# Attention, routed experts and a dense layer on one core: the first expert's first 128 slots are gathered within attention, and two of its h tiles take those slots in the slot chain

## The chip, the cores and the metric

The kernel runs on one core of a Trainium2 chip. The metric is device microseconds (us) of one execution, as a median of several runs. The engines are PE (TensorE: matmuls, and transposes by a matmul with the identity), DVE (VectorE), ACT (ScalarE), POOL (GpSimd) and SP (SyncE, which here issues DMAs). Each engine works through its own instructions in a fixed order and waits where an operand isn't there.

## The reference

All data is float32. There are 2304 tokens (4 sequences of 576), a model width of 512 (8 heads of 64), and 8 experts with an inner width of 1024.

```python
scores = (q @ k.T) / 8                     # per sequence and head
ret = (scores * gamma**(i - j) for i >= j) @ v
x = heads joined                           # 2304 x 512
logits = xn @ en.T / tau                   # rows and expert embeddings normalised
expert_idx = argmax(logits); gate = softmax(logits)[expert_idx]
for e in range(8):
    mask = expert_idx == e
    out[mask] = gate[mask] * (relu(x[mask] @ w1[e]) @ w2[e])
h = out @ w_in                             # second layer, 512 -> 2048
y = where(h > 0, h, exp(min(h, 0)) - 1) @ w_out
```

## The kernel before, in words

The program is one function, `tile_kernel`, in which the order on each engine is the order of the code: there is no scheduler. It has three stretches.

**Attention** runs over ten units `u` (0 to 9; `NU - 1` = 9 is the last one and is short). The output of a unit is one or two of the 18 token tiles `n` of 128 tokens. In a unit, PE makes the scores and values and a transposed output `xTp`; ACT copies it (`xT`, L395); PE turns it back and at the same time multiplies by the expert embeddings (`xa`, L444); DVE takes from `xa` the rows `xs`, which go by DMA to `xd` in DRAM, and the logits `lg` (L452 for the last tile, L460 for the others); ACT sums squares (`squares`, L478).

**Routing** is done in four groups of tiles, `GROUPS` = (first tile, count) = (0, 5), (5, 5), (10, 3), (13, 5). For each group `expert_steps` finds the winning expert of each token and its rank (`rp`, `pr`, L547) and `gate_steps` the gate (L588 to L599). `grouped` feeds a tile's steps in and `pump` deals them out between attention's instructions. For each tile `slots` (on POOL) makes a one-hot of the slot column (`o`, L609), one of the slot row (`Bt`, L610) and their products with token number and gate (`At`, L612). The first expert handled is that with the most tokens in the first two groups (`first`); its capacity is 342 slots, `CAPS[0]`, that of the others falls to 276.

**The slot chain** follows the last tile. PE multiplies `Bt` and `At` of all tiles into `pid` (token of each slot) and `pig` (gate of each slot): `begin` takes tiles 0 to 12, `finish` the last five. DVE reduces `pid` to `ids0` (shown as `ids`, L887), the list of the first expert's tokens, and POOL gathers their rows from `xd` with three indirect DMAs of 128, 128 and 96 rows (L945). Meanwhile `warm(8)` and `warm(4)` are matmuls on constants that nobody reads. `pig` then gives the gates (`gsl`), the three row blocks are scaled by them (`row`: blocks 0 and 2 on DVE L954, block 1 on ACT L956), PE transposes them (`tp`, L981), and they are split into a high and a low part, `xth` and `xtl`, because each fp32 product is made of three matmuls: high by high, low by high, high by low. Weights are split likewise: `ha`, `la` from the raw `ra` (first layer), `hb`, `lb` from `rb` (second layer); ACT makes the high part (L202), DVE the low (L207).

**The experts** are 64 steps `i`, eight an expert. `mm1` makes one h tile (128 of the 1024 inner units by up to 342 slots), L1003 for `i` = 0 and L233 for the others; ACT and DVE split it (`hh` L1008, `hl` L1009); `mm2` adds its product to the four accumulators `acc` (L1026, L1028). An h tile takes 12 matmuls in `mm1` and 12 in `mm2`, each as wide as the expert's capacity. After an expert the accumulators are copied into `ys` and sent to `yd`. The second layer follows, with products of summed and differenced blocks, and its own gathers and splits.

## Time and profile before

| what | value |
|---|---|
| time, median of 3 runs | 727.44 us (726.22 to 728.1) |
| the profiled execution's own time | 725.94 us |
| its span (first to last instruction) | 724.0 us |
| mean granted TensorE clock, of 1 | 0.992 |
| PE busy | 707.3 us, 98% of the span |
| PEld (weight loads) busy | 654.1 us, 90% |
| DVE busy | 589.3 us, 81% |
| ACT busy | 447.3 us, 62% |
| POOL busy | 260.5 us, 36% |

All start times in the rows are counted from the start of the span; the profiled execution's time is 1.94 us more than its span. The stretch of the change is from about 93 to 128 us: the last three attention units, the slot chain and the first h tiles.

### The profile page before, as it was taken

To read this page: it belongs to the slowest core of one execution; us is meant where nothing else is said; L and a number is where in the kernel's file an instruction comes from. 1 tells how busy PE (TensorE), PEld (TensorE's weight loads), DVE (VectorE), ACT (ScalarE), POOL (GpSimd) and SP (SyncE) were. 2 spreads that over 40 slices of the span, in tenths; PEclk is the share of its full clock that TensorE was granted. 3 is DMA by queue.
4 is the path that set the end of the run, shared out by engine and by line. 5 is a ranking of instruction groups with operands and counts; after the bars stand their busy time and mean duration, and the time that the engine had idled before them with its cause. 6 is when DMAs were issued, how large, how long until landed. Compare 5 with 4: busy or idle time off the path is not lost.

```text
span 724.0 us, 15526 instructions
## 1 busy us (share of the span) xinstructions
PE 707.3 (98%) x5940; PEld 654.1 (90%) x5940; DVE 589.3 (81%) x942; ACT 447.3 (62%) x690; POOL 260.5 (36%) x352
## 2 busy tenths in 40 slices
PE   8999979999999999999999999999999999999996
PEld 7988967999999999999989999889999989999985
DVE  4566789998888898789799999987779998777773
ACT  3443444656666666576777667776666778666572
POOL 3436643328483571003333222372112238111103
PEclk9999998999999999999999999999999999999998
DMA  7877656998999989795353311245211224211012
GB/s 211 230 218 223 170 171 211 314 348 271 359 284 326 327 270 307 239 348 159 106 176 109 110 59 59 69 165 167 67 59 58 84 90 142 64 59 59 29 30 87
DMA packets 101843, 123.66 MB, mean 171 GB/s; under 512 B 12250, under 2 KB 71934, under 8 KB 101766
## 3 DMA queue, kind: packets, MB, share of 16 engines
q1 hardware_dynamic: 98278, 112.62, 48.8%
q0 software_dynamic: 3104, 9.83, 3.8%
q8 instruction: 47, 0.77, 0.4%
q10 hardware_dynamic: 384, 0.19, 0.1%
q14 instruction: 30, 0.25, 0.1%
HBM read 99.78 MB, written 22.85 MB: 169 GB/s over the span
## 4 chain that ended last, share of the span: by engine, by line
PE 47%; issue 9%; POOL 1%; DMA 1%; DVE 0%; POOLq 0%; SPq 0%
PE o L233 20%; PE X L233 11%; PE Y L233 8%; PE h L233 3%; PE acc L1026 2%; PE acc L1028 1%; POOL out_dram L1474 1%; DMA qa<-wd 1%; POOL qs L1261 0%; POOL qa L1262 0%; POOL qs L1263 0%; DVE la('q', 20)_9470 L207 0%; PE tp L981 0%; POOLq L1558 0%; POOL qs L1264 0%
## 5 line engine op out<-in xcount | busy, mean ns | idle before, releaser
L1261 POOL TENSOR_TENSOR qs<-qa 128x256 f32<-128x256 f32 x24 | 23.6, 982 | 240.6 <-DMA qa<-wd 44.9
L233 PE MATMUL h<-xth,ha 128*128 128x332 f32 (+7 forms) x252 | 74.4, 311 | 0.1
L1026 PE MATMUL acc<-hh,lb 128*128 128x342 f32 (+7 forms) x256 | 73.5, 303 | 0.0
L1026 PE MATMUL acc<-hh,hb 128*128 128x342 f32 (+7 forms) x256 | 73.5, 304 | 0.0
L233 PE MATMUL h<-xtl,ha 128*128 128x332 f32 (+7 forms) x252 | 72.3, 303 | 0.0
L1008 ACT ACTIVATE hh<-h 128x342 fp32r<-128x342 f32 (+7 forms) x64 | 27.3, 426 | 52.2 <-PE h L233 50.8
L1425 ACT ACTIVATE rA<-hA 128x768 f32<-128x768 f32 x24 | 20.3, 848 | 50.4 <-DVE hA L1418 50.4
L1410 DVE TENSOR_TENSOR u<-Y,m 128x384 f32<-128x384 f32 x48 | 26.6, 554 | 28.0 <-PE Y L233 25.9
L207 DVE TENSOR_TENSOR la<-ra,ha 128x1024 fp32r<-128x1024 f32 x32 | 39.2, 1224 | 12.4 <-ACT ha L202 12.3
L1026 PEld LDWEIGHTS acc<-hh,lb 128*128 128x128 f32 x256 | 48.3, 189 | 0.0
L1026 PEld LDWEIGHTS acc<-hh,hb 128*128 128x128 f32 x256 | 48.2, 188 | 0.0
L233 PEld LDWEIGHTS h<-xth,ha 128*128 128x128 f32 x252 | 47.5, 189 | 0.6 <-issue 0.3
L233 PEld LDWEIGHTS h<-xtl,ha 128*128 128x128 f32 x252 | 47.6, 189 | 0.0
L945 POOL DMA_INDIRECT row<-xd,idsp x21 | 24.0, 1144 | 64.8 <-ACT xth L986 52.7
L1028 PE MATMUL acc<-hl,hb 128*128 128x342 f32 (+7 forms) x256 | 46.6, 304 | 0.4 <-DVE hl L1009 0.4
L233 PE MATMUL h<-xth,la 128*128 128x332 f32 (+7 forms) x252 | 45.6, 303 | 0.0
L1474 POOL DMA_INDIRECT out_dram<-ob,idc x18 | 21.2, 1178 | 66.6 <-ACT ob L1471 63.8
L207 DVE TENSOR_TENSOR lb<-rb,hb 128x1024 fp32r<-128x1024 f32 x32 | 39.4, 1233 | 3.7 <-ACT hb L202 3.5
L1028 PEld LDWEIGHTS acc<-hl,hb 128*128 128x128 f32 x256 | 39.0, 188 | 0.9 <-DVE hl L1009 0.9
L233 PEld LDWEIGHTS h<-xth,la 128*128 128x128 f32 x252 | 38.5, 188 | 0.0
L1442 ACT CAST ghB<-hB 128x768 fp32r<-128x768 f32 x24 | 20.0, 835 | 26.9 <-DVE hB L1438 26.9
L348 DVE TENSOR_TENSOR A<-sc,mask 128x512 f32<-128x512 f32 x32 | 20.6, 686 | 19.3 <-PE sc L342 19.3
(1693 smaller groups left out, 2343.2 us busy)
## 6 DMA issues: line engine op xcount, KB each, us to landing
ra<-in_moe_w_dram SPq DMA_DIRECT2D x32, 512.0 KB, 5.4
rb<-in_moe_w_dram SPq DMA_DIRECT2D x32, 512.0 KB, 5.6
qb<-wd SPq DMA_DIRECT2D x48, 256.0 KB, 2.9
draw<-in_moe_w_in_dram SPq DMA_DIRECT2D x16, 512.0 KB, 5.8
...
```

The lines of the kernel that those rows point to most:

```text
L207: nc.vector.tensor_tensor(out=lo, in0=src, in1=hi.bitcast(F32), op=ALU.subtract)
L233: nc.tensor.matmul(o, l, r, start=first and n_ == 0, stop=last and n_ == len(seq) - 1, skip_group_check=True)
L348: return vec.tensor_tensor(out=t[:, :, :w], in0=sc[j][:, :, :w], in1=m.unsqueeze(1).to_broadcast([P, 4, w]), op=ALU.mult)
L945: pool.indirect_dma_start(out=t[:m].rearrange("p k w -> p (k w)"), out_offset=None, in_=xd[:, :], in_offset=bass.IndirectOffsetOnAxis(ap=i ...
L1008: nc.scalar.activation(out=hh, in_=hp[:, :c], func=AF.Relu)
L1026: nc.tensor.matmul(acc[d][:, :c], w[d][w_], hh, start=f == 0 and w_ == 0, stop=False)
L1028: nc.tensor.matmul(acc[d][:, :c], w[d][0], hl, start=False, stop=f == 7)
L1261: pool.tensor_tensor(out=S1, in0=A21, in1=A22, op=ALU.add)
L1410: vec.tensor_tensor(out=S_[nm], in0=S_["Y"], in1=S_["m1"], op=ALU.add)
L1425: nc.scalar.activation(out=Q[n]["r" + z], in_=Q[n]["h" + z], func=AF.Relu, scale=-1.0)
L1442: nc.scalar.copy(out=Q[n]["gh" + z], in_=Q[n]["h" + z])
L1474: ins = pool.indirect_dma_start(out=out[:, :], out_offset=bass.IndirectOffsetOnAxis(ap=idc[:, col:col + 1], axis=0), in_=ob, in_offset=None)
```

## The change

Of the first expert's 342 slots the first 128, `EARLY`, can be filled from the first ten token tiles alone (`TEARLY` = 10, the first two groups), which are ranked long before the last tile. The changed kernel treats them apart:

- In unit 8 (`LAST - 1`) POOL marks the tokens of these slots (`early_slots`), PE multiplies (`pea`, ten matmuls of 5 columns), DVE reduces to `idsa` and `gsla`, and POOL gathers 128 rows, `rowa`, from the part of `xd` that the first ten tiles fill (`early_ids`).
- In unit 9 ACT scales `rowa` by the gates, PE transposes it, ACT makes its high part `xtha` (`early_turn`), and DVE, in the slot chain, its low part `xtla`.
- The first weight block's parts `ha`, `hb`, `la`, `lb` are made within attention and no longer in the slot chain and after it; `lb` is made on POOL. The loads of decoded weights (`decode_load`) and of the second raw block (`load_b(2)`) are issued later.
- In the slot chain PE computes the h tiles 0 and 1 for these 128 slots (`early1`) and their products with the second layer's weights (`early2`) into one bank `acce`. These 48 matmuls of 128 columns stand where 8 of the constant matmuls stood, before `rp`, and around the last tiles of `pid` and `pig`; `warm(8)` and `warm(4)` become `warm(4)` and `warm(3)`. `acce` is copied to `sume`.
- After the slot chain only two row blocks are gathered, of 128 and 96 rows; block 1 is scaled on DVE and block 2 on ACT. The early columns of `xth` and `xtl` are copied from `xtha` and `xtla` by ACT. `mm1` and `mm2` for `i` = 0 and 1 work on columns 128 to 341 (214 instead of 342); at the end of the first expert DVE adds `sume` to `ys`.

```diff
 SHORT = [c for _, c, _ in UNITS].index(-1)
 GROUPS = [(0, 5), (5, 5), (10, 3), (13, 5)]
 NPART = 5
+TEARLY = sum(GROUPS[GFIRST])
+EARLY = P
+FEARLY = 2
+assert EARLY * NE <= TEARLY * P
...
-    def split_low(w, u):
+    def split_low(w, u, eng=nc.vector):
         hi, lo, src = w[u]
-        nc.vector.tensor_tensor(out=lo, in0=src, in1=hi.bitcast(F32), op=ALU.subtract)
+        eng.tensor_tensor(out=lo, in0=src, in1=hi.bitcast(F32), op=ALU.subtract)
         w[u] = (hi, lo)
...
+    ea = {}
+    def early_slots():
+        f18 = st.tile([P, 1], F32, name="f18")
+        sel = st.tile([P, TEARLY], BF16, name="sel")
+        ea["ae"] = st.tile([P, TEARLY, NPART], BF16, name="ae")
+        pool.tensor_scalar(out=f18, in0=first, scalar1=float(NT), scalar2=None, op0=ALU.mult)
+        for gi in range(GFIRST + 1):
+            g0, gn = GROUPS[gi]
+            pool.tensor_scalar(out=sel[:, g0:g0 + gn], in0=gt[gi]["h"][:, 0, :gn], scalar1=f18, scalar2=None, op0=ALU.is_equal)
+        pool.tensor_tensor(out=ea["ae"], in0=sel.unsqueeze(2).to_broadcast([P, TEARLY, NPART]), in1=parts[:, :TEARLY, :], op=ALU.mult)
+    def early_ids():
+        p_ = ea["p"] = ps.tile([P, NPART], F32, tag="qT", name="pea")
+        for n in range(TEARLY):
+            nc.tensor.matmul(p_, Bt[:, n, :], ea["ae"][:, n], start=n == 0, stop=n == TEARLY - 1)
+        with nc.allow_low_precision(reason="whole numbers below 2304"):
+            vec.tensor_reduce(out=idsa, in_=p_[:, :2], axis=AX.X, op=ALU.add)
+        t = ea["row"] = dec.tile([P, DM], F32, tag="dsq", name="rowa", bufs=2)
+        pool.indirect_dma_start(out=t, out_offset=None, in_=xd[:TEARLY * P, :],
+                                in_offset=bass.IndirectOffsetOnAxis(ap=idsa, axis=0))
+        vec.tensor_reduce(out=gsla, in_=p_[:, 2:], axis=AX.X, op=ALU.add)
...
+    def early_turn():
+        pt = ea["pt"] = ps.tile([P, KD, P], F32, tag="kT", name="pta")
+        for kk in range(KD):
+            nc.tensor.transpose(pt[:, kk, :], ea["row"][:, kk * P:(kk + 1) * P], ident)
+        ea["xt"] = [dec.tile([P, KD, P], F32R, tag="dsq", name="xtha", bufs=2), dec.tile([P, KD, P], F32R, tag="db1", name="xtla", bufs=3)]
+        nc.scalar.copy(out=ea["xt"][0], in_=pt)
+    def spare_tile(tag, nm):
+        return ld.tile([P, H, 2, D], F32, tag="l" + tag, name=nm, bufs=4 if tag == "v" else 3).rearrange("p h s d -> p (h s d)")[:, :EARLY]
+    def early1(f, low):
+        if not low:
+            ea["hp", f] = ps.tile([P, 512], F32, tag="sc1", name="hea0") if f == 0 else ps.tile([P, 2, 512], F32, tag="Y", name="hea1")[:, 0]
+        hp = ea["hp", f][:, :EARLY]
+        xh, xl = ea["xt"]
+        w = tiles_a(f)
+        for l, r in ((0, xl),) if low else ((0, xh), (1, xh)):
+            for kk in range(KD):
...
+    def early_parts(f):
+        hp = ea["hp", f][:, :EARLY]
+        hh, hl = (spare_tile(t, f"e{x}{f}") for x, t in zip("hl", "qk"))
+        ea["h", f] = [hh.bitcast(F32R), hl.bitcast(F32R)]
+        nc.scalar.activation(out=ea["h", f][0], in_=hp, func=AF.Relu)
+        return lambda: vec.scalar_tensor_tensor(out=ea["h", f][1], in0=hp, scalar=0.0, in1=hh, op0=ALU.max, op1=ALU.subtract)
+    def early2(f, low):
+        if f == 0 and not low:
+            ea["acc"] = ps.tile([P, 2, 512], F32, tag="X", name="acce")[:, 0]
+        hh, hl = ea["h", f]
+        w = tiles_b(f)
+        for d in range(KD):
+            for w_, r in ((0, hl),) if low else ((0, hh), (1, hh)):
+                nc.tensor.matmul(ea["acc"][:, d * EARLY:(d + 1) * EARLY], w[d][w_], r, start=f == 0 and not low and w_ == 0 and d == 0,
+                                 stop=low and f == FEARLY - 1, skip_group_check=True)
+    def early_sum():
+        ea["sum"] = xr.tile([P, KD, EARLY], F32, name="sume")
+        vec.tensor_copy(out=ea["sum"], in_=ea["acc"].rearrange("p (k m) -> p k m", k=KD))
...
     held = None
+    LAST = NU - 1
     RANKED = 1 + [sum(GROUPS[GFIRST]) - 1 in ns for _, _, ns in UNITS].index(True)
     for u in range(NU):
         ns = UNITS[u][2]
...
+        if u == LAST:
+            nc.scalar.activation(out=ea["row"], in_=ea["row"], func=AF.Copy, scale=gsla)
         if held is not None:
             grouped(held)
+        if u == LAST - 1:
+            early_slots()
         if before is not None:
             xrows(before)
         if u < NU - 1 and u != SHORT:
         transposes(u + 1, 1)
         load(u + 3 if u else 2, "q" if u else "v", copied.get((u + 1, 1, "k")))
         if u == NU - 2:
+            split_of("a", 0, rawa[0], 1024, wa)
+        values(u)
+        load(u + 3, "k" if u else "q", copied[u, "x"])
+        if u == LAST - 1:
+            early_ids()
+        if u == LAST:
+            early_turn()
             decode_load(0)
...
         if before is not None:
             grouped(before)
+        if u == LAST - 1:
+            split_of("b", 0, rawb[0], 1024, wb)
         if u == NU - 1:
             while live:
...
         scores(u + 1, 0)
+        if u == LAST - 1:
+            split_low(wa, 0)
         xrows(ns[0], 2 if u == RANKED else 0)
         held = ns[0]
         for _ in range(8):
             if ready:
                 slots(*ready.pop(0))
+        if u == LAST - 1:
+            split_low(wb, 0, pool)
         if u < NU - 1:
             pump(1 if u == NU - 2 else 24, 0)
...
-    split_of("a", 0, rawa[0], 1024, wa)
+    early1(0, False)
     while live:
         pump(100, 0)
     while ready:
...
     steps(ge, 99)
+    vec.tensor_tensor(out=ea["xt"][1], in0=ea["pt"], in1=ea["xt"][0].bitcast(F32), op=ALU.subtract)
     steps(ge, 1)
     begin(pid, 0, 2)
+    early1(0, True)
+    early1(1, False)
+    low = early_parts(0)
...
     next(fi)
+    low()
     begin(pig, 2, NPART)
-    warm(8)
+    early1(1, True)
+    early2(0, False)
+    early2(0, True)
     next(fi)
+    row0 = {}
+    for j, m in ((1, P), (2, -(-(CAPS[0] - 2 * P) // 16) * 16)):
+        row0[j] = dec.tile([P, DM], I32, tag="db1", name=f"row0_{j}", bufs=3).bitcast(F32).rearrange("p (k w) -> p k w", k=KD)
+        pool.indirect_dma_start(out=row0[j][:m].rearrange("p k w -> p (k w)"), out_offset=None, in_=xd[:, :],
+                                in_offset=bass.IndirectOffsetOnAxis(ap=ids0[:m, j:j + 1], axis=0))
     while next(gg) != STEP:
         pass
     next(gg)
+    low = early_parts(1)
+    early2(1, False)
+    warm(4)
     next(fi, None)
     for _ in gg:
         pass
-    for _ in finish(pig, 2, NPART, gsl, gsl0):
+    fi = finish(pig, 2, NPART, gsl, gsl0)
+    next(fi)
+    low()
+    for _ in fi:
         pass
-    warm(4)
+    early2(1, True)
+    warm(3)
+    m0 = CAPS[0] - 2 * P
+    vec.tensor_scalar(out=row0[1], in0=row0[1], scalar1=gsl0[:, 1:2], scalar2=None, op0=ALU.mult)
+    nc.scalar.activation(out=row0[2][:m0], in_=row0[2][:m0], func=AF.Copy, scale=gsl0[:m0, 2:3])
...
         def weigh(j):
             m = fetched(key)[j]
             x = r[j][:m]
-            if early and j != 1:
-                vec.tensor_scalar(out=x, in0=x, scalar1=gates(j)[:m, :], scalar2=None, op0=ALU.mult)
-            else:
-                nc.scalar.activation(out=x, in_=x, func=AF.Copy, scale=gates(j)[:m, :])
+            nc.scalar.activation(out=x, in_=x, func=AF.Copy, scale=gates(j)[:m, :])
...
-        if (key, j) == (0, 1):
-            vec.tensor_copy(out=h_, in_=pt[:, :, :m])
-        else:
-            nc.scalar.copy(out=h_, in_=pt[:, :, :m])
+        nc.scalar.copy(out=h_, in_=pt[:, :, :m])
...
+    def columns(i, key):
+        return slice(EARLY if i < FEARLY else 0, cap(key))
...
         hp = pm.tile([P, 512], F32, tag="tp" if key == "x" else "h", name=f"h{i}", bufs=2)
         xh, xl = xt[key]
-        c = cap(key)
+        c = columns(i, key)
         if i:
-            several(hp[:, :c], [(w[kk], (xh[:, kk, :], xl[:, kk, :])) for kk in range(KD)], True, True)
+            several(hp[:, c], [(w[kk], (xh[:, kk, c], xl[:, kk, c])) for kk in range(KD)], True, True)
...
-                nc.tensor.matmul(acc[d][:, :c], w[d][w_], hh, start=f == 0 and w_ == 0, stop=False)
+                nc.tensor.matmul(acc[d][:, c], w[d][w_], hh, start=f == 0 and w_ == 0, stop=False, skip_group_check=True)
         for d in range(KD):
...
+            nc.tensor.matmul(acc[d][:, c], w[d][0], hl, start=False, stop=f == 7, skip_group_check=True)
...
-            nc.sync.dma_start(out=yd[:, :, bass.ds(ra(), c)], in_=ys)
+                nc.scalar.copy(out=ys[:, d, :], in_=acc[d][:, c])
+            if key == 0:
+                vec.tensor_tensor(out=ys[:, :, :EARLY], in0=ys[:, :, :EARLY], in1=ea["sum"], op=ALU.add)
+            nc.sync.dma_start(out=yd[:, :, bass.ds(ra(), cap(key))], in_=ys)
...
-    gather_expert(0)
+    rows[0] = row0
...
-    lows = [xpose(0, 0), xpose(0, 1)]
+    lows = [xpose(0, 1), xpose(0, 2)]
     t = pm.tile([P, 512], F32, tag="acc1", name="warmx")
     for _ in range(3):
         nc.tensor.matmul(t, lowb, oneb.unsqueeze(1).to_broadcast([P, 4, P]), start=True, stop=True)
-    for low in lows + [xpose(0, 2)]:
+    for low in lows:
         low()
+    nc.scalar.copy(out=xt[0][0][:, :, :EARLY], in_=ea["xt"][0].bitcast(F32))
+    nc.scalar.copy(out=xt[0][1][:, :, :EARLY], in_=ea["xt"][1].bitcast(F32))
     load_b(1)
     load_a(2)
     decode_load(2)
-    split_b(0)
+    load_b(2)
     for _ in go:
```

On ACT, in the last two attention units and up to the slot chain, the order before was (`sq` is a sum of squares, `xT_8` and `xT_9` are the copies of units 8 and 9, `ex` the exponentials of the third group's gates):

```order
L395 COPY xT_8_2196<-xTp_2075 128x512
L395 COPY xT_8_2198<-xTp_2075 128x512
L478 ACTIVATE sq_2200,ss_2019<-xs_2135 128x512
L586 ACTIVATE ex_2061<-ex_2061 128x24
L478 ACTIVATE sq_2267,ss_2019<-xs_2227 128x512
L395 COPY xT_9_2296<-xTp_2248 128x4x64
L395 COPY xT_9_2298<-xTp_2248 128x4x64
L478 ACTIVATE sq_2300,ss_2019<-xs_2274 128x512
```

and it is now (line numbers are those of the changed kernel):

```order
L208 CAST ha_2172<-ra_1928 128x1024
L403 COPY xT_8_2207<-xTp_2080 128x512
L403 COPY xT_8_2209<-xTp_2080 128x512
L486 ACTIVATE sq_2226,ss_2024<-xs_2147 128x512
L208 CAST hb_2228<-rb_1939 128x1024
L594 ACTIVATE ex_2066<-ex_2066 128x24
L819 ACTIVATE rowa<-rowa,gsla 128x512
L486 ACTIVATE sq_2299,ss_2024<-xs_2257 128x512
L403 COPY xT_9_2328<-xTp_2279 128x4x64
L403 COPY xT_9_2330<-xTp_2279 128x4x64
L765 CAST xtha<-pta 128x512
L486 ACTIVATE sq_2344,ss_2024<-xs_2306 128x512
```

The two splits `ha` and `hb`, the scaling of `rowa` and the cast `xtha` have come between them; the copies `xT_9` of the last unit now stand behind the scaling of `rowa`, which needs the gathered rows.

On POOL, from the last tiles' slot tables of the third group (`o_12`, `Bt`, `At`) to the first expert's gathers, the order before was:

```order
L609 TENSOR_SCALAR o_12_2243<-ct,hf_2148 128x24
L610 TENSOR_SCALAR Bt<-ct,hf_2148 128x128
L612 TENSOR_TENSOR At<-o_12_2243,parts 128x48
L612 TENSOR_TENSOR At<-o_10_2235,parts 128x72
L612 TENSOR_TENSOR At<-o_11_2239,parts 128x72
L612 TENSOR_TENSOR At<-o_12_2243,parts 128x72
L945 DMA row_0_2470<-xd,ids_77 128x512
L945 DMA row_1_2472<-xd,ids_77 128x512
L945 DMA row_2_2474<-xd,ids_77 96x512
```

and now, with the early gather shown first:

```order
L745 TENSOR_TENSOR ae<-sel,parts 128x50
L755 DMA rowa<-xd,idsa 128x512
L620 TENSOR_TENSOR At<-o_8_2049,parts 128x72
L620 TENSOR_TENSOR At<-o_9_2053,parts 128x72
L617 TENSOR_SCALAR o_10_2265<-ct,hf_2160 128x24
```

and, five slot-table operations further on:

```order
L617 TENSOR_SCALAR o_12_2273<-ct,hf_2160 128x24
L618 TENSOR_SCALAR Bt<-ct,hf_2160 128x128
L620 TENSOR_TENSOR At<-o_12_2273,parts 128x48
L213 TENSOR_TENSOR lb_2229<-rb_1939,hb_2228 128x1024
L620 TENSOR_TENSOR At<-o_10_2265,parts 128x72
L620 TENSOR_TENSOR At<-o_11_2269,parts 128x72
L620 TENSOR_TENSOR At<-o_12_2273,parts 128x72
L999 DMA row_1_2505<-xd,ids_77 128x512
L999 DMA row_2_2507<-xd,ids_77 96x512
```

The gather of `rowa` stands ahead of the slot tables of the third group, and the split `lb`, which DVE made after the slot chain, between these tables and the last three `At`.

On DVE, from the maximum (`m`) over the last group's scores to its ranks (`rk`), the order before was:

```order
L518 TENSOR_REDUCE m_2337<-sc_2336 128x5
L520 TENSOR_TENSOR oh<-sc_2336,m_2337 128x40
L547 TENSOR_TENSOR pr_2356<-rp_2343,oh 128x40
L482 TENSOR_SCALAR y_2373<-ss_2019 128x5
L566 TENSOR_REDUCE rk<-pr_2356 128x5
L485 TENSOR_SCALAR y_2373<-y_2373 128x5
```

and it is now:

```order
L526 TENSOR_REDUCE m_2387<-sc_2386 128x5
L528 TENSOR_TENSOR oh<-sc_2386,m_2387 128x40
L948 TENSOR_TENSOR xtla<-pta,xtha 128x512
L555 TENSOR_TENSOR pr_2407<-rp_2394,oh 128x40
L490 TENSOR_SCALAR y_2440<-ss_2024 128x5
L574 TENSOR_REDUCE rk<-pr_2407 128x5
L493 TENSOR_SCALAR y_2440<-y_2440 128x5
```

The low part `xtla` has come between `oh` and `pr`, the product that waits for PE's ranks `rp`. Two more pieces are new on DVE further down: the low part of h tile 0 (128x128) ahead of `p`<-`pid`, and that of h tile 1 ahead of `p`<-`pig`; `la` has moved from behind the scaling of block 0 to unit 9, ahead of `xs` of tile 15.

## Rows read from the trace of the kernel before

**Rows 1.** Windows of the steady expert stretch: busy time of each engine, granted clock, DMA share.

```profile
150.00:180.00 30.00, 30.00 (x202) 29.70 (x201) 27.21 (x45) 17.90 (x30) 19.28 (x23) 1.00 0.91 307
```

**Rows 2.** Windows of one microsecond in the slot chain: busy times, then granted clock.

```profile
105.00:106.00 1.00, 0.00 (x0) 0.00 (x0) 1.00 (x6) 0.46 (x1) 0.00 (x0) 0.79 0.43 148
108.00:109.00 1.00, 1.00 (x4) 0.34 (x3) 0.74 (x4) 0.21 (x1) 0.91 (x1) 0.50 0.00 0
113.00:114.00 1.00, 0.99 (x8) 0.76 (x9) 0.75 (x2) 0.79 (x2) 0.00 (x0) 1.00 0.10 37
```

**Rows 3.** Timeline from the last tile to the first gather: start, duration, engine, line, operation.

```profile
100.33 0.65 ACT L395 COPY xT<-xTp 128x256 f32<-128x256 f32 x2 [1.37 <-PE xTp L389]
100.76 1.47 PE L444 MATMUL xa<-rhsx,xT 128*64 128x144 f32 x16 [0.49 <-ACT xT L395]
101.60 0.16 DVE L599 TENSOR_TENSOR gate<-gate,parts 128x3 f32<-128x3 f32 x1
102.28 0.22 DVE L452 TENSOR_REDUCE lg<-xa 128x8 f32<-128x64 f32 x1
104.34 0.20 DVE L547 TENSOR_TENSOR pr<-rp,oh 128x40 f32<-128x40 f32 x1 [0.53 <-PE rp L537]
107.20 0.20 DVE L887 TENSOR_REDUCE ids<-p 128x3 int32<-128x48 f32 x1
107.70 1.21 POOL L945 DMA_INDIRECT row<-xd,ids  x1 [4.41 <-DVE r L580]
```

**Rows 4.** Timeline from the constant matmuls to the first h tile.

```profile
107.47 3.61 PE L796 MATMUL warm<-Bt,lowb 128*128 128x512 bf16 x8
...
110.87 0.51 PE L876 MATMUL pig<-At,Bt 128*128 128x72 bf16 x5
...
111.97 0.48 DVE L954 TENSOR_SCALAR row<-row,gsl 128x512 f32<-128x512 f32 x1
112.36 1.22 DVE L207 TENSOR_TENSOR la<-ra,ha 128x1024 fp32r<-128x1024 f32 x1
112.77 0.72 ACT L956 ACTIVATE row<-row,gsl 128x512 f32<-128x512 f32 x1 [4.56 <-DMA row<-xd,ids]
112.88 0.42 PEld L981 LDWEIGHTS tp<-ident,row 128*128 128x128 f32 x4 [0.70 <-issue]
...
113.83 0.48 DVE L954 TENSOR_SCALAR row<-row,gsl 96x512 f32<-96x512 f32 x1 [0.25 <-DMA row<-xd,ids]
...
115.69 0.89 PE L1003 MATMUL h<-xth,ha 128*128 128x342 f32 x4 [0.54 <-ACT xth L986]
```

**Rows 5.** Timeline of PE at two widths, the first of eight evenly spaced matmuls and what follows them.

```profile
117.67 0.32 PE L233 MATMUL h<-xth,ha 128*128 128x342 f32 x1
...
118.93 0.79 PE L233 MATMUL h<-xth,la 128*128 128x342 f32 x4
...
322.79 0.28 PE L1026 MATMUL acc<-hh,hb 128*128 128x276 f32 x1
...
323.80 0.68 PE L1028 MATMUL acc<-hl,hb 128*128 128x276 f32 x4
```

**Rows 6.** Gathers: issue to landing of all 24 (us), and median of the first expert's three.

```profile
DMA to landing us min/median/max: 3.3/5.1/8.2
row<-xd,ids POOLq DMA_INDIRECT x3, 3.5
```

**Rows 7.** Timeline: the same DVE operation without and with a POOL operation beside it.

```profile
48.73 0.16 DVE L492 SCALAR_TENSOR_TENSOR y<-y,r 128x5 f32<-128x5 f32 x1
51.21 2.04 POOL L286 TENSOR_TENSOR ks<-k,ct 128x512 f32<-128x512 f32 x2
52.31 0.97 DVE L492 SCALAR_TENSOR_TENSOR y<-y,r 128x5 f32<-128x5 f32 x1
344.43 0.74 POOL L1262 TENSOR_TENSOR qa<-qa 128x256 f32<-128x256 f32 x1
```

**Rows 8.** Timeline of POOL: first and last of the third group's nine slot-table operations.

```profile
95.59 0.34 POOL L609 TENSOR_SCALAR o<-ct,hf 128x24 bf16<-128x24 f32 x1 [2.06 <-DVE r L580]
98.73 0.26 POOL L612 TENSOR_TENSOR At<-o,parts 128x48 bf16<-128x48 bf16 x1
```

More of the change, by code (lines that the diff above doesn't have):

```diff
@@ L110, in tile_kernel @@
     gsl0 = cp.tile([P, 3], F32, name="gsl0")
+    idsa = cp.tile([P, 1], I32, name="idsa")
+    gsla = cp.tile([P, 1], F32, name="gsla")
     ohf = cp.tile([P, NE], F32, name="ohf")
@@ L238, in tile_kernel @@
     actx = ctx.enter_context(ExitStack())
+    xctx = ctx.enter_context(ExitStack())
+    xr = xctx.enter_context(tc.tile_pool(name="xr", bufs=1, side="right"))
     st = actx.enter_context(tc.tile_pool(name="st", bufs=1))
@@ new lines, in early1 @@
+    def early1(f, low):
[6 more added lines that the diff above has]
+            for kk in range(KD):
+                nc.tensor.matmul(hp, w[kk][l], r[:, kk, :], start=not low and l == 0 and kk == 0, stop=low and kk == KD - 1)
@@ L933, in fetched, with gather @@
         return [m if key == "x" else -(-m // 16) * 16 for _, m in subs(key)]
-    def gather(key, idx, gates, early=False):
+    def gather(key, idx, gates):
         r = []
         for j, m in enumerate(fetched(key)):
-            if early:
-                t = dec.tile([P, DM], I32 if j else F32, tag="db1" if j else "dsq", name=f"row0_{j}", bufs=3 if j else 2)
-                t = (t.bitcast(F32) if j else t).rearrange("p (k w) -> p k w", k=KD)
-            else:
-                t = local(key).tile([P, KD, P], F32, tag=f"row{j}", name=f"row{key}_{j}", bufs=1)
+            t = local(key).tile([P, KD, P], F32, tag=f"row{j}", name=f"row{key}_{j}", bufs=1)
             pool.indirect_dma_start(out=t[:m].rearrange("p k w -> p (k w)"), out_offset=None, in_=xd[:, :],
@@ L952, in weigh @@
             x = r[j][:m]
[L953 to L956 removed]
+            nc.scalar.activation(out=x, in_=x, func=AF.Copy, scale=gates(j)[:m, :])
         weighs[key] = weigh
[L959 to L963 removed]
     def gather_expert(e):
         if e < NE:
[L967 to L968 removed]
+            gather(e, lambda j: idsp[:, e, j:j + 1], lambda j: gslp[:, e, j:j + 1])
     xt = {}
@@ L974, in xpose @@
             return
-        if j == 0:
+        if key not in xt:
             w = CH if key == "x" else CAPS[0]
@@ L1018, in mm2 @@
     def mm2(i, f, key, w, ra):
-        c = cap(key)
+        c = columns(i, key)
         if f == 0:
```

29 lines of the change are left out of this document (10 added, 19 removed).

## The prediction

> **What bounds the kernel now.** I read the windows first. In the steady expert stretch PE is busy for all 30.00 us of 30.00, at granted clock 1.00, and the next engine, DVE, for 27.21 [rows 1]. So PE's matmuls set the time there, and fewer columns save time. The stretch of the change is different: one window of the slot chain has no PE work at all, and the granted clock falls to 0.50 (1.2 GHz) until it is back at 1.00 in 113 to 114 [rows 2]. There a chain of small steps sets the end. The timeline shows it: ACT's copy `xT` at 100.33, PE's `xa` at 100.76, the last tile's logits `lg` on DVE at 102.28, the ranks' product `pr` at 104.34, the token list `ids` at 107.20, the first gather at 107.70 [rows 3]. Then come the landings (ACT starts on block 1 at 112.77 and DVE on block 2 at 113.83, each released by its gather), the transposes, and the first `h` matmul at 115.69 [rows 4]. The constant matmuls hang beside this chain. From `h` on PE is the bound again. So the change is worth the PE time saved behind `h`, minus what the start of `h` moves by.
>
> **Term 1, the narrowed tiles: minus 2.5 us.** Two h tiles of 12 + 12 matmuls go from 342 to 214 columns, 48 in all. Eight matmuls of 342 columns take from 117.67 to 118.93, 0.157 each; eight of 276 take from 322.79 to 323.80, 0.126 each [rows 5]. The slope is 0.031 over 66 columns, so 214 columns would take 0.157 - 128 x 0.00047 = 0.097. But each matmul also needs a weight load of 128 columns, and the four of `tp` took 0.42, or 0.105 each [rows 4]. The gain is 48 x 0.060 = 2.9 by the slope and 48 x 0.052 = 2.5 by the loads. I take 2.5, since PEld is nearly full in this stretch already (29.70 of 30.00, [rows 1]).
> The Trainium skill, page "TensorE: Matmul & The Clock Gate", section "LDWEIGHTS (loading the stationary operand)", gives a load as columns / 1.2 ns, so 107 ns for 128 columns whatever the matmul's width; by it the gain would be 48 x 0.050 = 2.4. The trace's 0.105 agrees with it, while the slope alone would speak for 2.9.
>
> **Term 2, two gathers instead of three: minus 0.75.** The last block now comes with the second gather. Block 1's scaling began at its landing, 112.77, block 2's at 113.83 [rows 4], so the landing is 1.06 earlier. Block 2 is now scaled on ACT (0.72) and not on DVE (0.48) [rows 4], which costs 0.24; the `warmx` matmuls, which now stand behind the last transposes, may end a little after the cast `xth`, 0.07 by my estimate. -1.06 + 0.24 + 0.07 = -0.75.
>
> **Term 3, what DVE has more to do on the chain to `ids`: plus 0.35.** `xtla` (128x512) takes about 0.6, half of what `la` takes for twice the width (1.22, [rows 4]). It falls into the 0.53 us in which `pr` waits for `rp` [rows 3], so some 0.1 sticks out. The low part of h tile 0 (128x128) stands ahead of `p`<-`pid`: about 0.25, a quarter of the 0.48 for 512 columns [rows 4] plus the 0.16 that the smallest DVE operations take [rows 7]. `idsa` and `gsla` (two small reduces) and `la` (1.22, [rows 4]) go into unit 9, where DVE waits for PE; they cost nothing as long as `lg` isn't bound by DVE, which is the next term.
>
> **Term 4, `lg` of the last tile is late: plus 2.2.** Two things delay it; the later one counts, not the sum.
> (a) ACT. `rowa` is scaled ahead of `xT_9`, and PE's transposes of `rowa` stand ahead of `xa` too. `idsa` needs the ten small matmuls behind unit 8's values; I put it at 95.9, just behind the ranks of the third group, whose POOL work starts at 95.59 [rows 8]. POOL then issues at 96.3, the first expert's gathers landed after a median of 3.5 [rows 6], so 99.8 to 99.9. Scaling takes 0.72 [rows 4], `sq` about 0.5 (an estimate, from that 0.72 for the same width), and `xT_9` starts at about 101.1 instead of 100.33: +0.8. If the rows land early, `la` on DVE still leaves +0.4.
> (b) POOL and DVE. The gather holds POOL until 97.5 (1.21, [rows 3]); two `At` and three times `o`, `Bt`, `At` follow. The latter took 3.40 (95.59 to 98.99, [rows 8]). With a wait beside DVE's `la` until about 98.0 and 0.57 for the two `At`, `lb` starts at 102.0. It was never on POOL. The nearest row is a POOL TENSOR_TENSOR with two SBUF inputs on 128x512, two in 2.04 [rows 7], so 2.0 for 128x1024. DVE's own 1.22 [rows 4] is the lower bound, four of 128x256 at 0.74 [rows 7] the upper, 2.96. `lb` ends at about 104.0 (103.2 to 105.0).
> On DVE the third group's gate steps stand ahead of `lg`, and two of them (L599, the first at 101.60, [rows 3]) multiply two SBUF operands. With everything in front of them a little later they come at 102.1 and 102.5, just when `lb` has begun. Such small DVE operations took 0.16 alone but 0.97 beside a POOL operation of two SBUF inputs, and the DVE one ended at 53.28, with POOL's at 53.25 [rows 7]: it waited for POOL's to end. So these gate products wait until 104.0, and `lg` comes at 104.4 to 104.8 instead of 102.28. I take +2.2 (1.4 to 3.2 by the bounds of `lb`). Queued behind the waiting product on DVE are `lg`, the argmax and the whole chain to `ids`; for that wait PE's `rp` and POOL's gathers.
>
> **What costs nothing, and its cover.** The 48 early matmuls: 24 stand in place of `warm(8)`, with `warm(4)`. At full clock these take 24 x 0.105 + 4 x 0.213 = 3.4 us: 0.425 is what a constant matmul of 512 columns took at clock 0.50, eight from 107.47 to 110.87 [rows 4], and 0.213 its half. The room is the same 3.4 us, and there are 0.8 us more: the gates were there at 111.97, when DVE began to scale block 0, and the rows that are now the last landed at 112.77 [rows 4]. Without this cover each further microsecond on PE comes in full (rival B). The gates' chain to `gsl` has that slack as well. The later weight and decode loads, the copy `sume`, the copies of `xtha`, `xtla` and the addition to `ys` lie beside PE's matmuls. ACT and DVE are freed of `ha`, `hb`, `la`, `lb` around 112 to 118.
>
> **The sum.** `h` starts at 115.69 - 0.75 + 0.35 + 2.2 = 117.5, 1.8 later; term 1 gives back 2.5. Net 0.7 us: 725.2 against the profiled execution's own 725.94. That execution lies 1.5 us under the median of the three runs, 727.44; so as a median I predict 726.7. About 0.3% (2.2 us, so below 725.3 or above 729.6) is what a measurement of this kernel can tell from no change. With the bounds of `lb` and of term 1 the forecast's own range is 725.3 to 727.8.
>
> **The rivals.**
> A, `lb` misses the gate products: POOL reaches it half a microsecond later than I have it, or the gates are through. Then only the ACT wait (+0.8) is left, and the net gain is 2.5 + 0.75 - 0.35 - 0.8 = 2.1: 725.3, and 724.6 to 724.9 if the rows land early too. For it: my start of `lb` and that of the gate products lie within 0.5 us. Against it: both follow the same tiles, and POOL was never slower in [rows 8] than I assume. Chance 0.27; about two thirds of it is faster by over 0.3%.
> B, the clock: PE's work in the slot chain runs at 1.2 GHz, as `warm` did at 0.50 [rows 2], because PE still waits for `oh` and `pid`'s last tables. The 24 matmuls, at 0.105 to twice that, and 4 constant ones at 0.425 take 4.2 to 6.7 us in 3.4 us of room; minus the 0.8 of slack, 0 to 2.5 comes on top: up to 729.2. For it: the idle window is still there. Against it: matmuls on `rowa` now stand in the gap before `rp` and before `pid`'s last tables. Chance 0.12.
> C, on the other side: `rowa` lands as gathers do beside the expert stretch's traffic, up to 8.2 after issue with 5.1 in the middle of all [rows 6]. Up to 1.4 us more than 3.5 is free, under term 4 (b); beyond that ACT holds `xT_9`, PE holds `xa`, and each microsecond counts. At 8.2 `lg` is 5.5 late, +3.3 to the sum: 729.9. It decides (slower by over 0.3%) from a landing of about 8 us. For it: `xd` writes and loads run at that time. Against it: the three like it took 3.5. Chance 0.07.
> D, the change doesn't do what it says: DVE's `hl` and not PE sets the pace of the narrow tiles, and the gain of term 1 shrinks to about 2.0, 727.2. DVE has little else there, so 0.04.
>
> **How the numbers follow.** Forecast 0.50, A 0.27, B 0.12, C 0.07, D 0.04. Faster by over 0.3%: two thirds of A and a little of the forecast's lower end, 0.25. Slower: C's and B's upper ends and something of the forecast's upper bound, with the spread of a median of few runs, 0.14. The rest, 0.61, within 0.3%. The range 724.7 to 728.8 takes in A and most of B.
>
> **What would show it.** Term 1: spacing of the 214-column matmuls, 0.105. Term 2: the first `h` 2.1 after the second gather lands. Term 4: `lb` on POOL at about 102 for 2.0, a gate product of over 1 us beside it, `lg` at 104.4 to 104.8. Rival A: `lg` at about 103 and short gate products. B: granted clock at 0.5 while `hea` and `acce` run. C: ACT's scaling of `rowa` after 102. The prediction is wrong if `h` starts before 116.5 or after 119, or if the spacing isn't 0.097 to 0.105.

## The result, and the profile after

The changed kernel takes 734.62 us (median of 4 runs, 734.22 to 735.2) against 726.83 for the kernel before beside it (725.15 to 728.1, 4 runs): ratio 1.0109 [1.0086, 1.0133]. It is slower by about 1.1%, outside the predicted 724.7 to 728.8. The profiled execution took 734.51 us with a span of 732.6, so 8.6 us are to be found in spans (before: 724.0). The medians differ by 7.8, since the profiled execution of before lies 0.9 under its median.

The first rows show the end of attention and the last tile in the kernel after, to be read against [rows 3]:

```profile
98.52 1.21 POOL L755 DMA_INDIRECT rowa<-xd,idsa  x1 [2.01 <-DVE gsla L757]
99.86 0.42 DVE L356 TENSOR_TENSOR A<-sc,ctbig 128x256 f32<-128x256 f32 x1 [1.57 <-PE xa L452]
100.20 1.23 DVE L213 TENSOR_TENSOR la<-ra,ha 128x1024 fp32r<-128x1024 f32 x1
100.30 1.35 POOL L617 TENSOR_SCALAR o<-ct,hf 128x24 bf16<-128x24 f32 x1
...
102.19 0.72 ACT L819 ACTIVATE rowa<-rowa,gsla 128x512 f32<-128x512 f32 x1 [1.69 <-DVE lh L467]
104.69 2.35 POOL L213 TENSOR_TENSOR lb<-rb,hb 128x1024 fp32r<-128x1024 f32 x1
104.82 2.25 DVE L598 TENSOR_SCALAR gate<-gate 128x3 f32<-128x3 f32 x1
107.53 0.16 DVE L607 TENSOR_TENSOR gate<-gate,parts 128x3 f32<-128x3 f32 x1
...
108.21 0.22 DVE L460 TENSOR_REDUCE lg<-xa 128x8 f32<-128x64 f32 x1
110.27 0.20 DVE L555 TENSOR_TENSOR pr<-rp,oh 128x40 f32<-128x40 f32 x1
113.33 0.20 DVE L982 TENSOR_REDUCE ids<-p 128x3 int32<-128x48 f32 x1
```

A gate step of three columns lasts 2.25 us and ends at 107.07, `lb` at 107.04. An `A` product on DVE (scores times decay, the last tile's attention) begins 0.13 after the end of the early gather.

The slot chain in the kernel after, to be read against [rows 4] and [rows 5]:

```profile
109.79 0.18 PE L535 MATMUL rp<-oh,lowb 128*128 128x40 bf16 x1 [2.63 <-DVE oh L528]
...
114.71 0.41 PE L794 MATMUL acce<-eh,hb 128*128 128x128 f32 x1
114.93 0.41 PE L794 MATMUL acce<-eh,lb 128*128 128x128 f32 x1
...
120.28 0.51 PE L971 MATMUL pig<-At,Bt 128*128 128x72 bf16 x5
...
121.09 0.23 DVE L982 TENSOR_REDUCE gsl<-p 128x3 f32<-128x72 f32 x1
121.36 0.72 ACT L1019 ACTIVATE row<-row,gsl 86x512 f32<-86x512 f32 x1 [6.50 <-DVE gsl L982]
121.49 0.91 PE L887 MATMUL warm<-Bt,lowb 128*128 128x512 bf16 x3
122.56 0.93 PE L1081 MATMUL tp<-ident,row 128*128 128x128 f32 x8 [0.15 <-PE warm L887]
...
124.33 0.70 PE L1103 MATMUL h<-xth,ha 128*128 128x214 f32 x4 [0.20 <-ACT xth L1083]
...
125.77 0.27 PE L239 MATMUL h<-xth,ha 128*128 128x214 f32 x1
125.87 0.28 PE L239 MATMUL h<-xtl,ha 128*128 128x214 f32 x1
125.98 0.27 PE L239 MATMUL h<-xth,ha 128*128 128x214 f32 x1
```

Windows of the kernel after (busy time of PE, PEld, DVE, ACT, POOL, then granted clock), to be read against [rows 1] and [rows 2]:

```profile
107.00:108.00 1.00, 0.15 (x2) 0.08 (x2) 0.83 (x6) 0.00 (x0) 0.04 (x1) 1.00 1.07 367
111.00:112.00 1.00, 1.00 (x9) 1.00 (x8) 1.00 (x6) 0.28 (x1) 0.00 (x0) 0.72 0.33 123
115.00:116.00 1.00, 1.00 (x7) 1.00 (x6) 0.83 (x6) 0.00 (x0) 0.83 (x1) 0.50 0.39 78
120.00:121.00 1.00, 1.00 (x9) 0.72 (x8) 0.17 (x1) 0.00 (x0) 0.00 (x0) 0.50 0.00 0
122.00:123.00 1.00, 0.85 (x6) 0.48 (x5) 0.45 (x1) 0.08 (x1) 0.00 (x0) 1.00 0.00 0
150.00:180.00 30.00, 30.00 (x201) 29.71 (x200) 27.72 (x46) 18.46 (x33) 13.39 (x18) 1.00 0.93 314
```

PE idles for 2.63 before 109.79; from then on it is busy, and its granted clock falls to 0.72 in 111 to 112 and stays at 0.50 (1.2 GHz) from 112 to 121. `acce`'s matmuls start every 0.213, and the last `pig` matmuls, which give the gates, stand behind them in PE's order. The ACT row says that block 2 waited 6.50 for `gsl`, not for its gather.

Cutting both spans at the same events gives the whole difference:

| stretch | before | after | difference |
|---|---|---|---|
| start to `xs` of tile 13 | 93.45 | 95.73 | +2.28 |
| to `lg` of the last tile | 8.83 | 12.48 | +3.65 |
| to `ids` | 4.92 | 5.12 | +0.20 |
| to the first `h` | 8.49 | 11.00 | +2.51 |
| to the last `yd` store (end of the experts) | 229.69 | 227.41 | -2.28 |
| to the 13th scatter of the second layer | 366.37 | 368.56 | +2.19 |

The sum is 8.55. The third and fourth lines together are the slot chain; the last line lies more than 200 us behind the change, where nothing was edited. Its rows, first before, then after:

```profile
345.38 0.58 SPq L1033 DMA_DIRECT2D yd<-ys  x1
...
711.75 0.99 POOL L1474 DMA_INDIRECT out_dram<-ob,idc  x1 [37.49 <-ACT ob L1471]
```

```profile
351.74 0.57 SPq L1135 DMA_DIRECT2D yd<-ys  x1
...
720.30 0.99 POOL L1580 DMA_INDIRECT out_dram<-ob,idc  x1 [37.79 <-ACT ob L1577]
```

### The profile page after: what moved, and what is told of

It is laid out like the page before. It is cut to its first block, busy times and chain, and to the rows that moved or that the text cites. A ratio compares the mean times of both kernels' runs of the same rounds, so it can differ in the third digit from the quotient of the medians.

```text
span 732.6 us, 15651 instructions
## 1 busy us (share of the span) xinstructions
PE 715.4 (98%) x5993; PEld 662.1 (90%) x5993; DVE 589.5 (80%) x945; ACT 450.6 (62%) x696; POOL 261.2 (36%) x357
## 4 chain that ended last, share of the span: by engine, by line
PE 49%; issue 7%; POOL 1%; DMA 0%; DVE 0%; POOLq 0%; SPq 0%
PE o L239 22%; PE X L239 12%; PE Y L239 9%; PE h L239 3%; PE acc L1126 2%; PE acc L1128 1%; POOL out_dram L1580 1%; DMA qa<-wd 0%; POOL qs L1366 0%; DVE la('q', 21)_9695 L213 0%; PE tp L1081 0%; POOLq L1664 0%; POOL qs L1363 0%; POOL qa L1364 0%; POOL qs L1365 0%
## 5 line engine op out<-in xcount | busy, mean ns | idle before, releaser
L239 PE MATMUL h<-xth,ha 128*128 128x332 f32 (+8 forms) x252 | 74.0, 311 | 0.1
L1126 PE MATMUL acc<-hh,lb 128*128 128x312 f32 (+8 forms) x256 | 72.9, 302 | 0.0
L1126 PE MATMUL acc<-hh,hb 128*128 128x312 f32 (+8 forms) x256 | 72.8, 302 | 0.0
L239 PE MATMUL h<-xtl,ha 128*128 128x332 f32 (+8 forms) x252 | 71.8, 303 | 0.0
L1108 ACT ACTIVATE hh<-h 128x332 fp32r<-128x332 f32 (+8 forms) x64 | 27.1, 423 | 50.2 <-PE h L239 48.7
L1128 PE MATMUL acc<-hl,hb 128*128 128x312 f32 (+8 forms) x256 | 46.3, 303 | 0.3 <-DVE hl L1109 0.2
L239 PE MATMUL h<-xth,la 128*128 128x332 f32 (+8 forms) x252 | 45.6, 303 | 0.0
```

The lines of the kernel that those rows point to most:

```text
L239: nc.tensor.matmul(o, l, r, start=first and n_ == 0, stop=last and n_ == len(seq) - 1, skip_group_check=True)
L1108: nc.scalar.activation(out=hh, in_=hp[:, c], func=AF.Relu)
L1126: nc.tensor.matmul(acc[d][:, c], w[d][w_], hh, start=f == 0 and w_ == 0, stop=False, skip_group_check=True)
L1128: nc.tensor.matmul(acc[d][:, c], w[d][0], hl, start=False, stop=f == 7, skip_group_check=True)
```

## The experiments

Ratios are against the kernel before, run beside each, with a 95% interval. The theory was: the clock at 1.2 GHz in the slot chain and the `lb` lock make the loss; rivals were the early gather itself and the stretch behind the experts. Two kernels were run again unchanged.

> The kernel before, unchanged, as a control. In the changed kernel's trace everything ahead of the change's stretch is late already: the rows xs of tile 13 come at 95.73 instead of 93.45 us, 1.4 of it from the first loads on and 1.2 from a stretch at 80 to 85 in which DVE waits beside POOL. Theory A, that this is how single executions differ: here xs of tile 13 lies anywhere between 93 and 96, and the time within 725 to 728.5. Theory B, that the change causes it: 93.45 within 0.3 again.

The kernel before: 725.98 us (10 runs), 1.0007 [0.9994, 1.0019]. `xs` of tile 13 comes at 93.42, as theory B has it (in e8, below, at 93.42 again); the eleven profiles of changed kernels have 93.59 to 95.73. So the late start belongs to the changed kernels, by an amount that differs from execution to execution.

> The changed kernel, unchanged, as a control: 734.0 to 735.2 if its first four runs stand for it; lg of the last tile 11 to 12.5 us behind xs of tile 13 and the second layer, from the last store of yd to the first scatter of its last group, 368.6 against 366.4 in both traces of before. If that second-layer stretch varies by execution, it comes out at 366.4 here or in other runs; if it belongs to the program, it is 368.6 again.

The kernel after: 733.26 us (4 runs), 1.0093 [1.0078, 1.0109], a little under the 734.0 to 735.2 expected. Its profile has 94.90 in the table's first line, then 12.47 to `lg`, 5.44 to `ids`, 12.02 to `h`, and 368.63 in the second layer: the same losses, less at the start and 1.0 more in the slot chain.

**e1, `lb` earlier on POOL.**

```diff
+        if u == LAST - 1:
+            split_low(wb, 0, pool)
         for _ in range(8):
             if ready:
                 slots(*ready.pop(0))
-        if u == LAST - 1:
-            split_low(wb, 0, pool)
```

> The changed kernel with one move: lb stands on POOL ahead of the third group's slot tables, not behind them. Theory lock (a gate step on DVE waited 2.1 us for POOL's lb): lb now runs beside operations of DVE that read PSUM, the gate step takes 0.2, and lg of the last tile comes 2.0 earlier, 6.0 to 6.3 us behind before's becoming 3.8 to 4.2; the time falls from 734.6 to 732.6. Rival (DVE would have waited for xa of the last tile anyway, and the gate step only filled that): lg 0.3 earlier at most, 734.3.

730.24 us (725.77 to 732.51, 10 runs), 1.0044 [1.0022, 1.0066]. The timeline of e1, and then a window of it:

```profile
97.44 1.21 POOL L755 DMA_INDIRECT rowa<-xd,idsa  x1 [1.97 <-DVE gsla L757]
97.71 0.42 DVE L356 TENSOR_TENSOR A<-sc,ctbig 128x256 f32<-128x256 f32 x1 [0.50 <-PE sc L350]
...
99.39 2.34 POOL L213 TENSOR_TENSOR lb<-rb,hb 128x1024 fp32r<-128x1024 f32 x1 [0.74 <-ACT hb L208]
...
102.65 0.32 DVE L598 TENSOR_SCALAR gate<-gate 128x3 f32<-128x3 f32 x1
...
104.49 0.21 DVE L460 TENSOR_REDUCE lg<-xa 128x8 f32<-128x64 f32 x1
...
106.04 0.18 PE L535 MATMUL rp<-oh,lowb 128*128 128x40 bf16 x1 [0.81 <-DVE oh L528]
```

```profile
108.00:109.00 1.00, 1.00 (x11) 1.00 (x11) 0.96 (x5) 0.00 (x0) 0.00 (x0) 0.50 0.08 15
```

The gate step is back at 0.32, and from `xs` of tile 13 to `lg` takes 9.84 instead of 12.48. The clock still fell to 0.50 in this profile, from 108 to 117, so the lock and the clock are two losses. In this one kernel the time goes with the clock: of its ten runs three have a mean granted clock of 0.997 to 0.999 and take 725.8 to 726.7 us, seven have 0.988 to 0.991 and take 729.6 to 732.5.

**e2, PE filled before `rp`.** Ten constant matmuls of 512 columns behind the first early ones:

```diff
     early1(0, False)
+    fill = ps.tile([P, 2, 512], F32, tag="X", name="fill")[:, 0]
+    for _ in range(10):
+        nc.tensor.matmul(fill, lowb, Bt[:, 0:4, :].rearrange("p n q -> p (n q)"), start=True, stop=True)
```

> The changed kernel with 10 constant matmuls of 512 columns on PE between the first early matmuls and rp, where PE stood idle from 107.2 to 109.8. Theory clock (the early matmuls ran at granted clock 0.50 because of that idle time, and so took twice as long): the granted clock stays at 1.00 from 110 to 120, a 128-column matmul of acce takes 0.107 and not 0.213, the gates' last pig comes 2.5 to 3 us earlier, and the time falls to 732. Rival (the early matmuls wait for their operands el, not for the clock): clock up, but pig at most 0.5 earlier, 734.1 or more.

728.52 us (727.96 to 728.75, 6 runs), 1.0026 [1.0012, 1.0041]. The timeline of e2, and then a window of it:

```profile
111.27 0.27 PE L794 MATMUL acce<-eh,hb 128*128 128x128 f32 x1
111.38 0.28 PE L794 MATMUL acce<-eh,lb 128*128 128x128 f32 x1
...
114.51 0.32 PE L974 MATMUL pig<-At,Bt 128*128 128x72 bf16 x5
```

```profile
112.00:113.00 1.00, 1.00 (x11) 1.00 (x11) 0.72 (x4) 0.33 (x2) 0.69 (x2) 1.00 0.00 0
```

The clock holds, and `acce`'s matmuls start every 0.11. From `ids` to the first `h` takes 7.24 instead of 11.00, with `lb` still locking the gate step (2.80). All six runs have a mean granted clock of 0.997 or more. More work on PE made the kernel 4.7 us faster than c1, a larger fall than expected.

**e3, no gather by index.** `rowa` comes by a plain copy of 128 consecutive rows of `xd`, so the gather's place on POOL is gone. The token list isn't used, and the early rows aren't those of the expert.

```diff
-        pool.indirect_dma_start(out=t, out_offset=None, in_=xd[:TEARLY * P, :],
-                                in_offset=bass.IndirectOffsetOnAxis(ap=idsa, axis=0))
+        nc.sync.dma_start(out=t, in_=xd[:P, :])
```

> The changed kernel with the early gather replaced by a plain copy of 128 consecutive rows issued by SP, so the early rows are not those of the expert's tokens. Theory gather (while POOL makes the gather's descriptors, from 98.5 to 99.7, DVE's masked scores A of the last unit can't start): A starts 0.0 to 0.1 after its scores, 1.2 earlier, and lg of the last tile 1.1 to 1.6 earlier; the time 733.2. Rival (A waits for something else on PE): A again 1.2 after its scores, 734.5.

730.85 us (725.94 to 731.48, 10 runs), 1.0048 [1.0029, 1.0067]. `A` comes 2.95 after `xs` of tile 13 instead of 4.13, `lb` begins at 100.40, the gate step at 102.00 takes 0.80, and the way to `lg` is 9.89. But in e1 and e2 `A` comes as early, 3.06 and 3.07 after `xs` of tile 13, with the gather in place, and `lb` moved as well. So what the gather itself costs isn't shown by e3. The runs fall apart as in e1: three at a mean granted clock of 0.996 or more take up to 728.1, the other seven (0.989 to 0.991) 729.9 and more.

**e4, the two new tiles elsewhere.** The stretch behind the experts was 2.2 us longer in every profile of the changed kernel. The two new 32-byte tiles `idsa` and `gsla` in the constant pool move the tiles behind them by 64 bytes, those of the second layer too. Here they are taken from another pool, so that the others stand at the addresses of before.

```diff
-    idsa = cp.tile([P, 1], I32, name="idsa")
-    gsla = cp.tile([P, 1], F32, name="gsla")
...
+    idsa = st.tile([P, 1], I32, name="idsa")
+    gsla = st.tile([P, 1], F32, name="gsla")
```

> The changed kernel with the two small tiles idsa and gsla taken from attention's own pool, so that the weights' and the second layer's tiles stand at the SBUF addresses of before again and not 64 bytes further. Theory address: the second layer takes 366.4 and not 368.6, the time falls by 2.2, from 734.6 to 732.4. Rival (the second layer's 2.2 us come from something else, as the place of its instructions): 368.6 again, no change in time.

731.79 us (4 runs), 1.0079 [1.0064, 1.0094]. Its last `yd` store and 13th scatter:

```profile
351.08 0.57 SPq L1135 DMA_DIRECT2D yd<-ys  x1
...
717.50 0.99 POOL L1580 DMA_INDIRECT out_dram<-ob,idc  x1 [37.50 <-ACT ob L1577]
```

366.42 between them, as before, and a median 1.5 us under that of c1.

**e8, the kernel before with two unused tiles.** The opposite test: nothing but the shift (and two small writes at the start).

```diff
     gsl0 = cp.tile([P, 3], F32, name="gsl0")
+    idsa = cp.tile([P, 1], I32, name="idsa")
+    gsla = cp.tile([P, 1], F32, name="gsla")
+    nc.gpsimd.memset(idsa, 0)
+    nc.gpsimd.memset(gsla, 0.0)
```

> The kernel before with two small unused tiles (idsa and gsla, each written once at the start) in its constant pool, which puts the weights' and the second layer's tiles 64 bytes further, as in the changed kernel; nothing else. Theory address: the second layer takes 368.6 and not 366.4, the time rises by 2.2, from 726.1 to 728.3. Rival (it needs more of the change than the addresses): 366.4 and no change in time.

728.46 us (11 runs), 1.0037 [1.0025, 1.0049]. The same two rows of e8:

```profile
345.36 0.58 SPq L1037 DMA_DIRECT2D yd<-ys  x1
...
713.91 0.99 POOL L1478 DMA_INDIRECT out_dram<-ob,idc  x1 [37.79 <-ACT ob L1475]
```

368.55, while everything up to `h` is where it was (115.57). The shift alone costs 2.2 us.

**e5, e6, e7: the repairs together.** e5 has `lb` early as e1 and 4 fill matmuls as e2; e6 is e5 with the tiles of e4; e7 is e6 with 8:

```diff
-    for _ in range(4):
+    for _ in range(8):
         nc.tensor.matmul(fill, lowb, Bt[:, 0:4, :].rearrange("p n q -> p (n q)"), start=True, stop=True)
```

> lb ahead of the slot tables, and 4 constant matmuls of 512 columns between the first early matmuls and rp. Lock and clock theories together: lg 9.8 to 10 us behind xs of tile 13, granted clock 1.00 in the slot chain, gates (gsl) 9.1 to 9.4 behind lg instead of 12.9; the time 2.3 to 2.6 below the run with the filling alone, 726. If four matmuls are too few to hold the clock: gsl 12.9 behind lg and 730.

> The same with idsa and gsla in attention's pool. Theory address: another 2.2 us less than that run, 723.9, so faster than before by 2. Rival: as that run.

> The changed kernel with lb ahead of the slot tables, 8 constant matmuls between the first early matmuls and rp, and idsa and gsla in attention's pool. With 4 of them the granted clock held in most executions and fell in some. Clock theory: with 8 it holds in nearly all, gsl 9.1 to 9.8 behind lg, runs within 1.5 us of each other, median 725.5 to 726.5. If the clock depends on other things than the matmuls there, some runs stay at 730 as with 4.

e5: 731.52 us (727.57 to 732.91, 7 runs), 1.0055 [1.0036, 1.0075], where 726 was expected: two runs near 728, at a mean granted clock of 0.998 and 0.999, and five from 730.4 up, at 0.991 to 0.995. Its profile shows 7.77 from `ids` to `gsl`, as long as without fill (7.76). e6: 726.47 us (12 runs), 1.0012 [0.9995, 1.0030], where 723.9 was expected: nine runs at or below 727.3 (0.996 to 0.999) and three from 729.7 up (0.988 to 0.990); its profile has 4.01 there. e7: 724.85 us (724.58 to 725.51, 11 runs), 0.9981 [0.9973, 0.9990]: 1.3 us faster than the kernel before (726.18), the best version found. With four fill matmuls the clock held in some runs and fell in others; with eight the mean granted clock was 0.997 or more in all eleven runs. The gain isn't what a held clock alone would give the kernel before, whose own clock falls to 0.50 in the slot chain [rows 2]: of 96 of its runs, seven have a mean granted clock of 0.998 or 0.999, with a median of 725.92 against 726.11 for the others. The timeline of e7:

```profile
98.41 2.35 POOL L211 TENSOR_TENSOR lb<-rb,hb 128x1024 fp32r<-128x1024 f32 x1 [0.74 <-ACT hb L206]
...
101.66 0.34 DVE L596 TENSOR_SCALAR gate<-gate 128x3 f32<-128x3 f32 x1
103.78 0.21 DVE L458 TENSOR_REDUCE lg<-xa 128x8 f32<-128x64 f32 x1
...
109.58 0.20 DVE L985 TENSOR_REDUCE ids<-p 128x3 int32<-128x48 f32 x1
113.59 0.23 DVE L985 TENSOR_REDUCE gsl<-p 128x3 f32<-128x72 f32 x1
114.90 0.72 ACT L1022 ACTIVATE row<-row,gsl 86x512 f32<-86x512 f32 x1 [4.13 <-DMA row<-xd,ids]
116.82 0.59 PE L1106 MATMUL h<-xth,ha 128*128 128x214 f32 x3
```

Here block 2 is released by its gather again, and `h` follows 1.92 later. `h` starts 1.13 after that of before, and the narrow tiles give back about twice that.

**e9 and e10, other shifts.** e7 with one and with three unused 32-byte tiles in the constant pool (`pad0`, then `pad1` and `pad2` as well):

```diff
+    pad0 = cp.tile([P, 1], F32, name="pad0")
+    nc.gpsimd.memset(pad0, 0.0)
```

> The version with lb ahead, 8 constant matmuls and before's addresses, plus one small unused tile in the constant pool: the weights' and the second layer's tiles stand 32 bytes further than in before. Theory boundary (places 64 bytes apart differ since one lies better against a boundary of 64 bytes or more): 32 bytes gives neither of the two, the second layer takes another time than 366.4 and 368.6, or one of the two with a step at some distance. Rival (only the distance from before's own place counts, smoothly): about 367.5.

> The same with three such tiles, 96 bytes further. Boundary theory: as with 32 bytes if the boundary is 64 bytes; not as with 32 if it is 128 or more. Rival: more than 368.6, about 369.7.

e9: 727.57 us (10 runs), 1.0018 [1.0008, 1.0028]; e10: 725.53 us (10 runs), 0.9998 [0.9988, 1.0007]. From the last `yd` store to the 13th scatter took 366.38 in e7 (no shift), 368.22 in e9 (32 bytes), 365.79 in e10 (96 bytes), and 368.55 in e8 (64 bytes, on the kernel before). So it is no matter of more or less, as the rival in e9 had it, and no simple rule of alignment comes out of four points. (e10's median is still 0.7 above e7's; its profile is 1.07 later already at `xs` of tile 13.)

## Why the prediction was wrong

By its own signs the prediction is wrong: `h` starts at 124.33, past the limit of 119, and the narrow matmuls stand 0.111 apart, just outside 0.097 to 0.105.

**Term 1, right, with the gain put a little too high.** The 214-column matmuls start at 125.77, 125.87, 125.98: 0.111 apart, where 0.105 was taken from the `tp` loads. 48 x (0.157 - 0.111) = 2.2, and the stretch behind `h` became shorter by 2.28. The Trainium skill, page "TensorE: Matmul & The Clock Gate", section "LDWEIGHTS (loading the stationary operand)", gives columns / 1.2 ns for a load, and the estimate from it was a gain of 2.4; the measured 0.111 lies nearer to its 107 ns than to the 0.097 of the slope. The 128-column matmuls of `acce` in e2 stand 0.11 apart as well, with PEld busy throughout (1.00 in 112 to 113), so here the spacing follows the weight loads and not the columns.

**Term 2, right where the gather binds.** In e7 `h` starts 1.92 after the second gather released ACT, where 2.1 was expected, and `ids` to `h` is 7.24 against 8.49 before: -1.25 for the -0.75 predicted. In the changed kernel itself the landing no longer bound anything, because the gates came later.

**Term 3.** `lg` to `ids` grew by 0.20, and by 0.52 in c1 (0.35 predicted).

**Term 4, the right mechanism, sized too small.** `lb` did catch DVE's gate steps: counted from `xs` of tile 13, `lb` was put at 8.55 and began at 8.96; it was to take 2.0 and took 2.35. The step that it blocked was the `TENSOR_SCALAR` ahead of the gate products, not one of the products, so three pairs of steps were still to come when `lb` ended, and `lg` followed 1.17 after that end, not 0.48. 0.41 + 0.35 + 0.69 = 1.45, which is 3.65 - 2.2, and 3.65 lies above the term's upper bound of 3.2. (What the prediction calls gate products, L607 after, are subtractions; they do have two SBUF operands.) e1 shows the lock's own worth: without it the way to `lg` is 2.3 shorter than in e2, which like e1 has its `A` early. Where `A` is late, e6 and e4 give 1.6.
The Trainium skill, page "SBUF — State Buffer", section "Who interferes with whom", says that a DVE `tensor_scalar` in its two-port mode and a GpSimd operation lock each other out for a whole instruction, whoever issues first. The trace agrees as far as it goes: 2.25 us for a step of 0.17 before (100.98), ending 0.03 after `lb`; in which mode the step ran it doesn't show. In e2 the step is recorded from 102.07, ahead of `lb` at 102.49, and still ends 0.03 after it, so the recorded starts don't tell which of the two blocks. The prediction had passed over the `TENSOR_SCALAR` step because it looked only for two SBUF operands.

**The step that failed most: that the 48 early matmuls cost nothing, "At full clock these take 24 x 0.105 + 4 x 0.213 = 3.4 us".** They ran at half clock. Rival B had the mechanism and a chance of 0.12. Its reason against, that matmuls on `rowa` stand in the gap before `rp`, didn't hold: they end by 107.15, PE then waits 2.63 us for `oh`, and the granted clock is 0.72 in 111 to 112 and 0.50 from then on. Term 4 makes that gap wider, but that isn't needed: the gap was 1.31 in c1 and 0.81 in e1, where `lb` no longer blocks the gate step, and in both profiles the clock fell. e2 and e7 show that with constant matmuls in the gap the same matmuls run at 1.00. The price was also too low. From `ids` to `h` the forecast was 7.74 (8.49 - 0.75) and 11.00 came, 3.26 more, where B's upper end was 2.5. The gates came 3.27 later, which minus the 0.8 of slack is 2.5 as priced; but the last four `acce` matmuls and `warm(3)`, in front of the first transposes, also began at half clock (`warm(3)` from 121.49 to 122.40), and `tp` waited for them. From the scaling of block 2 to `h` took 2.97, where the forecast had 2.17 (114.94 - 112.77): the remaining 0.8. In e7, at full clock, it took 1.92.

**Not in the prediction at all: the second layer, +2.19.** e4 takes it away, e8 brings it about in the kernel before with nothing else changed. The sentence that put all other parts of the change at nothing named loads, copies and an addition, and not that two new tiles move the addresses of others.

**Rivals A, C and D did not come.** `lb` did not miss the gate steps. `rowa` was scaled at 102.19, 3.67 after its gather began, waiting at the end for DVE's `lh` by the trace; C needed about 8. The narrow tiles kept PE's pace: PE was busy for 2.00 of 2.00 from 126 to 128, and the one wait for `hl` that follows (0.39 from start to start, 127.88 to 128.27) was there before as well (0.50, 120.68 to 121.18).

**What stays open.** The first 2.28 us, up to `xs` of tile 13: the other ten profiles of changed kernels have 0.1 to 1.5 there (median about 0.8 over all eleven), and no run was made for it alone. Addresses are a rival there too: the early pass's tiles `f18`, `sel` and `ae` stand in attention's own pool, ahead of other tiles of attention, and none of the runs takes that back. How the shift of addresses costs time is open as well, and so is why the clock held in three of e1's runs and not in the others.

With the forecast's 0.7 for the net change, the errors are: term 1 +0.2, term 3 -0.15, term 4 +1.45, clock +3.26, second layer +2.19, the start +2.28; together 9.2 on -0.7, so 8.5 of the 8.6 measured.
